# Sinkhorn attention and routed experts on one core: keys and scores of batches 2 to 4 issued in longer runs

## The chip, the core and the metric

The kernel runs on one NeuronCore of a Trainium2 chip. TensorE (PE) multiplies into PSUM, eight banks of 2 KB per partition; VectorE (DVE) and ScalarE (ACT) read PSUM and write SBUF, where operands live; GpSimd (POOL) works on SBUF and issues DMAs, and SyncE (SP) issues DMAs. Each engine takes its own instructions in order. The metric is the time of one execution on the device in microseconds (us), lower is better.

## The reference, cut to what matters

For each of 4 batches and 8 heads (768 positions, 64 dimensions, 8 blocks of 96), a normalised 8 x 8 matrix P sorts the blocks of keys and values; attention is then taken inside each block. The result, 3072 x 512, goes through 8 experts with weights from a Sinkhorn balance of the gate's logits.

```python
    for _ in range(5):
        P = P - np.max(P, axis=-1, keepdims=True)
        P = np.exp(P)
        P = P / (np.sum(P, axis=-1, keepdims=True) + 1e-09)
        P = P / (np.sum(P, axis=-2, keepdims=True) + 1e-09)
    k_sorted = np.einsum('bhij,bhjcd->bhicd', P, k_b).reshape(B, H, S, D)
    v_sorted = np.einsum('bhij,bhjcd->bhicd', P, v_b).reshape(B, H, S, D)
    scores = scale * np.matmul(q_b, k_sb.transpose(0, 1, 2, 4, 3))
    attn = np.exp(scores)                       # less the row's maximum
    attn = attn / (np.sum(attn, axis=-1, keepdims=True) + 1e-09)
    x = np.matmul(attn, v_sb)                   # then to 3072 x 512
    # experts: P from x @ w_gate, balanced 8 times over rows and columns
    for e in range(E):
        h = np.maximum(x @ w1[e], 0.0)
        out += P[:, e:e + 1] * (h @ w2[e])
```

## The kernel before, in words

The first batch (index 0 in the code) is done by its own code up to line 535. The other three go through `attention(bb, bank, plan)`, line 369: a generator that reads a string. Each word of the string is a step, and a step is one or more pieces joined by commas, a letter and a head pair (0 to 3):

- `q`, `queries` (174): turns a pair's queries on TensorE. Batch 2 (index 1) does it with 128*64 matmuls, one head into each half of the columns; batches 3 and 4 first have POOL reorder them into `qr`, two buffers (186), and use 128*128 matmuls. ACT copies the result to `qTs`; DVE does for pairs 2 and 3 of batch 2 and for pair 3 of batch 4 (193).
- `k`, `keys` (196): the sorted keys in two halves of three steps, each with one bank, 128*64 matmuls into both column halves; DVE copies each half to `kTs` (209).
- `s`, `scores` (218): four banks, 16 matmuls with 64 rows each, the two heads in the two row halves; ACT takes the exponent of each bank (234).
- `m`, `mix` (237): four banks of attention times sorted values (`vsb`); DVE takes reciprocals and products into `og` (247, 248).
- `t`, `turn` (252): turns `og` through one bank; DVE copies to `xtT` (258). `l`, `logits` (263): the gate. `x`: one subtraction of `sum_x(0)` on DVE (128).

All these matmuls are pinned in the order of the program on TensorE. The copies on DVE and ACT are not: the planner of the framework orders them by their data and gives each tile a bank of the pool `pa`, which has eight (547).

Between the steps TensorE works on the first expert for the batch before: `first_two` (556) yields a hidden step (four matmuls of 384 columns, one bank, Relu on ACT, 399) or half of an output tile (four matmuls of 512 columns into a bank that its second half shares, then a copy by ACT or DVE, 414). `run_both` and `weave` say how many of them follow each step. `sort_values` (162) makes the next batch's sorted values, two heads a step, and `hop` (155) sends them to `vsb` by eight DMAs, half on SP and half on POOL. `load_batch` (70) and `spread_r` (151) put the next batch's loads and its sort matrix on POOL.

After the attention the rest (lines 613 on) is the experts: the last two batches of expert 0 beside the balance, then experts 1 to 7.

Of the kernel before, what the change touches and what calls it, by code (L numbers as in the profile page):

```python
# [25 lines left out]
def kernel(  # L26
# [124 lines left out]
    def spread_r(bb):  # L151
        for _ in build_r(bb, nc.gpsimd, 4):
            pass

    def hop(bb, pieces=None):
        for eng, i, h0, n in pieces or [(nc.gpsimd if i % 2 and bb > 1 else nc.sync, i, 0, 8)
                                        for i in range(NB)]:
            (pin if bb == 0 else lambda ins: ins)(eng.dma_start(
                out=mkap(vsbt[bb % 2], [[VW, 96], [1, 65 * n]], off=i * 520 + 65 * h0),
                in_=vs[16 * i:16 * i + 16, :, h0:h0 + n].rearrange("p kk h d -> p kk (h d)")))  # L160

    def sort_values(bb, bank):
        for h in range(8):
            vps = bank([128, 384], F32)
            pin(nc.tensor.matmul(vps, Rt[bb][:, h].rearrange("p i c -> p (i c)"),
                                 vt[bb][:, h, :], start=True, stop=True))
            nc.scalar.copy(vs[:, :, h, 0:64], vps.rearrange("p (kk d) -> p kk d", d=64))
            if h % 2:
                yield
        hop(bb)  # L170
# [3 lines left out]
    def queries(bb, hp, bank):  # L174

        qps = bank([128, 6, 128], BF16)
        if bb < 2:

            for kk in range(6):
                for h in range(2):  # L180
                    pin(nc.tensor.matmul(qps[64 * h:64 * h + 64, kk, :],
                                         qt[bb][:, 2 * hp + h, kk * 64:kk * 64 + 64],
                                         Ibig, is_transpose=True, start=True, stop=True))
        else:
            qr = sp.tile([128, 6, 2, 64], BF16, name="qr", bufs=2)
            nc.gpsimd.tensor_copy(
                qr.rearrange("p kk h d -> p h kk d"),
                qt[bb][:, 2 * hp:2 * hp + 2].rearrange("p h (kk d) -> p h kk d", d=64))
            for kk in range(6):
                pin(nc.tensor.matmul(qps[:, kk, :], qr[:, kk].rearrange("p h d -> p (h d)"),  # L190
                                     Ibig, is_transpose=True, start=True, stop=True))
        qT[bb, hp] = sp.tile([128, 128, 6], BF16, name="qTs", bufs=4)
        (nc.vector.tensor_copy if bb == 1 and hp > 1 or bb == 3 and hp == 3 else nc.scalar.copy)(
            qT[bb, hp], qps.rearrange("p kk c -> p c kk"))

    def keys(bb, hp, bank):

        kT[bb, hp] = sp.tile([128, NB, 16, 6], BF16, name="kTs", bufs=4)
        for b in range(2):
            kps = bank([128, 3, 128], F32)  # L200
            for j in range(3):
                kk = 3 * b + j
                for h in range(2):
                    pin(nc.tensor.matmul(  # L204
                        kps[64 * h:64 * h + 64, j, :],
                        kt[bb][:, 2 * hp + h, kk * 64:kk * 64 + 64],
                        Rt[bb][:, 2 * hp + h].rearrange("p i c -> p (i c)"),
                        start=True, stop=True))
            nc.vector.tensor_copy(kT[bb, hp][:, :, :, 3 * b:3 * b + 3],
                                  kps.rearrange("p kk (i c) -> p i c kk", i=8))  # L210
# [7 lines left out]
    def scores(bb, hp, bank):  # L218

        for b in range(2):  # L220
            sps = [bank([128, 4, 96], F32) for h in range(2)]
            for j in range(4):
                i = 4 * b + j
                for h in range(2):
                    r = slice(64 * h, 64 * h + 64)
                    pin(nc.tensor.matmul(  # L226
                        sps[h][0:96, j, :],
                        kT[bb, hp][r, i].rearrange("p c kk -> p (c kk)"),
                        qT[bb, hp][r, 16 * i:16 * i + 16].rearrange("p c kk -> p (c kk)"),
                        start=True, stop=True))  # L230
            for h in range(2):
                if b == 0:
                    new_at(bb, hp, h)
                nc.scalar.activation(out=at[bb, hp, h][0:96, 4 * b:4 * b + 4],
                                     in_=sps[h][0:96], func=AF.Exp, scale=scale)
# [133 lines left out]
    def attention(bb, bank, plan):  # L369

        def step(what, hp):
            if what == "q":
                queries(bb, hp, bank)
            elif what == "k":
                keys(bb, hp, bank)
            elif what == "s":
                scores(bb, hp, bank)
            elif what == "t":
                turn(bb, hp, bank, nc.vector.tensor_copy)
            elif what == "x":  # L380
                next(x0)
            elif what == "l":
                logits(bb, bank, (0, 1, 2) if hp == 0 else (3,))
            else:
                for h in range(2):
                    mix(bb, hp, h, bank)

        for some in plan.split():
            for x in some.split(","):
                step(x[0], int(x[1]))  # L390
            yield
# [41 lines left out]
    with tc.tile_pool(name="ps0", bufs=4, space=bass.MemoryType.PSUM,  # L433
# [71 lines left out]
        for x in ("s00 k2 s01 k3 p s02 s03 m00 s10 m01 s11 m02 t00 m03 s12 m10 t01 s13 h00 m11 "  # L505
# [12 lines left out]
            elif x[0] == "g":  # L518
                b, g, t = *n, part[x[1:]]
# [26 lines left out]
    with ExitStack() as c2:  # L546
        pa = c2.enter_context(tc.tile_pool(name="pa", bufs=8, space=bass.MemoryType.PSUM,
                                           reuse_waits="tile"))
        bank1 = lambda shape, dt: pa.tile(shape, dt, name="bank", tag="bank")
        ebank = lambda: bank1([128, 512], F32)  # L550
        def by_turns(x, y):
            for a, b in ((x, y), (x, y)):
                yield next(a)
                yield next(b)

        def first_two():
            yield from hidden0(384, halves[1], ebank, range(2, 8))
            for c0, hTs in ((0, halves[0]), (384, halves[1])):
                o = [output0(c0, hTs, ebank, keep, (tt,)) for tt in range(3)]
                if c0 == 0:  # L560
                    yield from by_turns(o[0], o[1])
                    yield from o[2]
                else:
                    for one in o:
                        yield from one
            for c0 in (S, S + 384):
                hTs = mps.tile([128, 8, 384], BF16, name="hTs")
                yield from hidden0(c0, hTs, ebank)
                yield from output0(c0, hTs, ebank, keep)

        ex = first_two()

        def run(n):
            for _ in range(n):
                next(ex)

        def run_both(a, counts):
            for n in counts:
                next(a, 0)
                run(n)  # L580

        at1 = attention(1, bank1, "k0 k1 q0 q1 s0 k2 q2 k3 q3 s1 s2 s3 "
                                  "m0 m1,t0 m2,t1 m3,t2 t3,l0 l3")
        run_both(at1, (1, 1, 1, 0, 1, 0, 0, 1, 0, 1, 0, 2))
        load_batch(2, [(x, 0, 8) for x in "vkq"])
        spread_r(2)
        run_both(at1, (2, 1, 1, 1))
        run_both(sort_values(2, bank1), (1, 0, 1, 0, 1))
        run_both(at1, (1, 1))
        usual = "q0,q1,k0 q2,k1,s0 q3,k2,s1 m0 k3,s2 m1,t0 s3 m2,t1 m3 t2 t3,l0 l3"  # L590
        for bb, ns in ((2, (5, 3, 2, 4)), (3, (5, 4, 0, 5))):
            at1 = attention(bb, bank1, usual if bb == 3 else usual.replace(
                "q2", "q2,x0").replace("q3", "q3,x0").replace("t0", "t0,x0"))
            weave(at1, ex, 5, ns[0])
            if bb + 1 < B:
                load_batch(bb + 1, [(x, 0, 8) for x in "vkq"])
                spread_r(bb + 1)
            else:
                load_w1(1)
                sums = sum_w(1)  # L600
            weave(at1, ex, 3, ns[1])
            if bb + 1 < B:
                weave(sort_values(bb + 1, bank1), ex, 5, ns[2])
            else:
                for _ in sums:
                    pass
            weave(at1, ex, 4, ns[3])
        for _ in ex:
            pass
# [16 lines left out]
    def bank():  # L626
        return bk.tile([128, 512], F32, name="bk")
# [314 lines left out]
```

## Time and profile before

| | |
|---|---|
| median of 3 runs | 667.63 us (667.5 to 667.65) |
| profiled execution | 667.97 us |
| its span, first to last instruction | 666.2 us |
| TensorE busy | 658.0 us (99%), 5141 matmuls |
| DVE, ACT, POOL busy | 557.9 (84%), 300.3 (45%), 471.0 us (71%) |
| attention of batches 2 to 4 on TensorE | 36.13 us (first keys) to 106.68 us |
| experts after it | 106.68 us to the end |

The busy time of TensorE is the union of its matmuls' records; their ends are modelled, and a matmul's record is longer than the step from its start to the next one's. So work on TensorE is best read from starts. "128*64" in a row is the stationary operand: rows by columns of the array in use. A bracket at the end of a timeline row is the idle time ahead of it and what ended it.

### The profile page before, as it was taken

The numbers are of one execution on the slowest core, as the hardware profiler recorded it, in microseconds if no ns is written. First come the engines' busy times: TensorE is split into PE (matmuls) and PEld (weight loads), VectorE is DVE, ScalarE is ACT, GpSimd is POOL, SyncE is SP. The second block draws the span as 40 slices with busy tenths as digits, with TensorE's granted clock in tenths as the row PEclk, the third lists the DMA queues.
The fourth block names the chain that finished last, engine by engine and source line by source line (L and its number), as shares of the span: only waits on it lengthen the run. The fifth ranks groups of instructions, "written<-read, shape, count | busy, mean of one in ns | idle before, by whom it ended". The sixth has DMA issues, their size and how long they took to land.

```text
span 666.2 us, 13218 instructions
## 1 busy us (share of the span) xinstructions
PE 658.0 (99%) x5141; PEld 435.5 (65%) x5141; DVE 557.9 (84%) x1128; ACT 300.3 (45%) x535; POOL 471.0 (71%) x500
## 2 busy tenths in 40 slices
PE   7999999999999999999999999999999999999997
PEld 3766675554666666666666666666666666666666
DVE  6656876785888898998989898988998989898996
ACT  5775773476455443333334333433343334333430
POOL 4813353037897998898897999689886999646652
PEclk9999999999999999999999999999999999999999
DMA  9998964003041240033103040034003130001124
GB/s 188 172 220 143 150 110 64 1 1 63 1 64 16 49 64 1 0 64 44 21 1 64 1 64 2 1 63 64 1 1 65 16 50 1 1 0 62 68 95 159
DMA packets 33375, 36.96 MB, mean 55 GB/s; under 512 B 2112, under 2 KB 26400, under 8 KB 33312
## 3 DMA queue, kind: packets, MB, share of 16 engines
q0 software_dynamic: 26784, 27.03, 25.9%
q1 hardware_dynamic: 6416, 8.99, 4.3%
q8 instruction: 40, 0.66, 0.4%
q14 instruction: 23, 0.19, 0.1%
q10 hardware_dynamic: 112, 0.10, 0.1%
HBM read 52.45 MB, written 6.29 MB: 88 GB/s over the span
## 4 chain that ended last, share of the span: by engine, by line
PE 95%; DVE 2%; DMA 1%; ACT 0%; issue 0%; POOL 0%; ACTq 0%; DVEq 0%; POOLq 0%
PE bk L694 38%; PE oacc L781 38%; PE bk L397 3%; PE bank L406 3%; PE oacc L406 3%; PE bank L397 2%; PE bank L244 1%; PE pair L365 1%; PE bank L204 1%; PE bank L226 1%; PE bk L781 1%; PE bank L255 1%; DMA vsb<-vs 1%; PE bk L817 1%; DVE vs L283 0%; PE bank L190 0%
## 5 line engine op out<-in xcount | busy, mean ns | idle before, releaser
L746 DVE SCALAR_TENSOR_TENSOR osbl<-oacc,glog,osbl 128x256 f32<-128x256 f32 (+1 forms) x490 | 255.7, 524 | 27.9 <-PE oacc L781 18.2
L764 POOL TENSOR_TENSOR hs<-hT 128x512 bf16<-128x512 bf16 (+2 forms) x105 | 98.6, 951 | 72.3 <-DVE hT L712 72.2
L694 PE MATMUL bk<-xtT,w1e 128*128 128x512 bf16 x504 | 148.6, 379 | 0.0
L712 DVE CUSTOM_DVE_ANT_0 hT<-bk,p 128x512 bf16<-128x512 f32 x168 | 116.1, 691 | 26.7 <-PE bk L694 23.5
L781 PEld LDWEIGHTS <-hT 128*128 128x128 bf16 x996 | 97.4, 98 | 62.6 <-issue 0.2
L781 PEld LDWEIGHTS <-hs 128*128 128x128 bf16 x996 | 97.4, 98 | 61.2 <-issue 1.6
L781 PE MATMUL oacc<-w2e,hT 128*128 128x256 bf16 x796 | 119.7, 273 | 0.0
L717 ACT COPY p<-bk 128x512 f32<-128x512 f32 x84 | 49.3, 587 | 147.4 <-PE bk L694 147.0
L764 POOL TENSOR_TENSOR hs<-hs,hT 128x512 bf16<-128x512 bf16 (+2 forms) x105 | 99.6, 958 | 4.5 <-ACT hT L739 0.2
L764 POOL TENSOR_TENSOR hs<-hT,hs 128x512 bf16<-128x512 bf16 (+2 forms) x105 | 99.1, 952 | 4.7
L694 PE MATMUL bk<-xc,wc 128*128 128x512 bf16 x336 | 99.8, 379 | 0.0
L739 ACT ACTIVATE hT<-bk 128x512 bf16<-128x512 f32 x84 | 50.2, 597 | 96.1 <-PE bk L694 96.1
L781 PE MATMUL oacc<-w2e,hs 128*128 128x256 bf16 x612 | 91.8, 273 | 0.0
L694 PEld LDWEIGHTS <-w1e 128*128 128x128 bf16 x672 | 65.7, 98 | 12.1
L740 DVE SCALAR_TENSOR_TENSOR h<-bk,hT 128x512 bf16<-128x512 f32 x84 | 57.2, 681 | 3.9 <-ACT hT L739 3.9
L712 DVE CUSTOM_DVE_ANT_0 hT<-bk,u 128x512 bf16<-128x512 f32 x84 | 58.0, 690 | 2.5 <-PE bk L694 2.5
L721 ACT COPY u<-bk 128x512 f32<-128x512 f32 x84 | 49.2, 586 | 23.8 <-PE bk L694 23.2
L726 ACT COPY p<-bk 128x512 f32<-128x512 f32 x84 | 49.3, 587 | 23.4 <-PE bk L694 23.4
L694 PEld LDWEIGHTS <-wc 128*128 128x128 bf16 x504 | 49.3, 98 | 8.0 <-issue 0.2
L781 PE MATMUL oacc<-w2s,hs 128*128 128x256 bf16 x364 | 53.3, 272 | 0.0
L694 PE MATMUL bk<-xtT,wc 128*128 128x512 bf16 x168 | 50.0, 379 | 0.0
L694 PE MATMUL bk<-xc,w1e 128*128 128x512 bf16 x168 | 50.0, 379 | 0.0
(149 smaller groups left out, 791.4 us busy)
## 6 DMA issues: line engine op xcount, KB each, us to landing
w1e<-in_moe_w_dram POOLq DMA_DIRECT2D x7, 1024.0 KB, 8.1
w2e<-in_moe_w_dram POOLq DMA_DIRECT2D x7, 1024.0 KB, 8.9
out_dram<-osbl SPq DMA_DIRECT2D x23, 256.0 KB, 2.0
kvq<-in_v_dram POOLq DMA_DIRECT2D x3, 768.0 KB, 10.6
kvq<-in_k_dram POOLq DMA_DIRECT2D x3, 768.0 KB, 11.5
vsb<-vs SPq DMA_DIRECT2D x18, 97.5 KB, 4.6
kvq<-in_q_dram POOLq DMA_DIRECT2D x4, 384.0 KB, 10.2
kvq<-in_q_dram POOLq DMA_DIRECT2D x2, 768.0 KB, 20.2
```

The lines of the kernel that those rows point to most:

```text
L397: pin(nc.tensor.matmul(hps[:, 0:384], w1t[0][:, kk, fb * 128:(fb + 1) * 128], xtT[:, kk, c0:c0 + 384], start=(kk == 0), stop=(kk == 3)))
L406: pin(nc.tensor.matmul(oacc, hTs[:, fb, tt * 128:(tt + 1) * 128], w2t[0][:, fb, :], start=(fb == 0), stop=(fb == 7)))
L694: hold(nc.tensor.matmul(ps, wa[:, kk, :], xa[:, kk, :], start=(first and kk == 0), stop=(kk == 1), skip_group_check=True))
L712: nc.vector._custom_dve(TENSOR_ADD_SAT, out=out, in0=ps, in1=other, s0=TOP, s1=0.0)
L717: still(nc.scalar.copy(p1, u))
L721: still(nc.scalar.copy(u2, u))
L726: still(nc.scalar.copy(p5, v))
L739: still(nc.scalar.activation(out=c21, in_=u, func=AF.Relu))
L740: nc.vector.scalar_tensor_tensor(out=h3[e, p][:, i, :], in0=u, scalar=0.0, in1=c22, op0=ALU.max, op1=ALU.subtract)
L746: nc.vector.scalar_tensor_tensor(out=o, in0=ps, scalar=glog[:, t, e:e + 1], in1=o, op0=ALU.mult, op1=ALU.add)
L764: hold(nc.gpsimd.tensor_tensor(out=c, in0=a, in1=b, op=o))
L781: nc.tensor.matmul(ps, h[:, fb, :], w[:, fb, :], start=(first and fb == 0), stop=(fb == 3), skip_group_check=True)
```

## The change

The plans, the strings, are rewritten, and a few counts with them.

- Batch 2: one hidden step goes ahead of the first keys. Then the keys of all four pairs and two queries in one step; the other two queries and the scores of two pairs in one; the scores of the other two. Before, most pieces had a step of their own with expert work between.
- Of the first expert's first half tile row, the first halves of all three output tiles (`by_turns` now takes any number) stand ahead of the first mix, then the second halves; before, two tiles went in turns and the third after them. The counts behind the later steps and in the sorting of batch 3's values are lowered to fit, so that all in all as much expert work lies in each batch as before.
- Batches 3 and 4: keys of pairs 0 and 1 in a run, keys 2 and 3 followed by scores 0 and 1 in a run, scores 2 and 3 in a run after mix 1; mix 2 and mix 3 move back by a step and turn 3 follows mix 3 and turn 2 closer. A step `-` does nothing and only leaves its place to expert work. The `x` pieces go with the same letters as before.

What is computed, and by how many instructions, stays.

```diff
+            elif what == "-":
+                pass
...
-        def by_turns(x, y):
-            for a, b in ((x, y), (x, y)):
-                yield next(a)
-                yield next(b)
+        def by_turns(*some):
+            for _ in range(2):
+                for one in some:
+                    yield next(one)
...
                 if c0 == 0:
-                    yield from by_turns(o[0], o[1])
-                    yield from o[2]
+                    yield from by_turns(*o)
...
-        at1 = attention(1, bank1, "k0 k1 q0 q1 s0 k2 q2 k3 q3 s1 s2 s3 "
+        at1 = attention(1, bank1, "k0,k1,k2,k3,q0,q1 q2,q3,s0,s1 s2,s3 "
                                   "m0 m1,t0 m2,t1 m3,t2 t3,l0 l3")
-        run_both(at1, (1, 1, 1, 0, 1, 0, 0, 1, 0, 1, 0, 2))
+        run(1)
+        run_both(at1, (2, 2, 4))
         load_batch(2, [(x, 0, 8) for x in "vkq"])
         spread_r(2)
-        run_both(at1, (2, 1, 1, 1))
-        run_both(sort_values(2, bank1), (1, 0, 1, 0, 1))
-        run_both(at1, (1, 1))
-        usual = "q0,q1,k0 q2,k1,s0 q3,k2,s1 m0 k3,s2 m1,t0 s3 m2,t1 m3 t2 t3,l0 l3"
+        run_both(at1, (3, 1, 1, 1))
+        run_both(sort_values(2, bank1), (1, 0, 1, 0, 0))
+        run_both(at1, (1, 0))
+        usual = "q0,q1,k0,k1 q2,q3 k2,k3,s0,s1 -0 m0 m1,t0 s2,s3 t1 m2 m3,t2 t3,l0 l3"
```

## The prediction

> **What bounds the kernel now.** Times are in us, durations from the one profiled execution. I read the page first (busy shares, chain), then TensorE's timeline around the attention of batches 2 to 4, then what ACT and DVE do beside it.
>
> ```profile
> PE 658.0 (99%) x5141; PEld 435.5 (65%) x5141; DVE 557.9 (84%) x1128; ACT 300.3 (45%) x535; POOL 471.0 (71%) x500
> ...
> PE 95%; DVE 2%; DMA 1%; ACT 0%; issue 0%; POOL 0%; ACTq 0%; DVEq 0%; POOLq 0%
> ```
>
> TensorE is the bound: 99% busy, 95% of the chain. So what the change does to TensorE's order counts in full, a saved switch as well as a new wait. Two stretches of TensorE's timeline (start, length, engine, line, operation), from batch 3 and from batch 2, show what it saves:
>
> ```profile
> 64.27 0.53 PE L204 MATMUL bank<-R,kvq 128*64 128x128 bf16 x12
> 64.73 0.82 PE L397 MATMUL bank<-xtT,w1e 128*128 128x384 bf16 x4
> 65.39 0.50 PE L190 MATMUL bank<-Ibig,qr 128*128 128x128 bf16 x6
> 65.82 0.53 PE L204 MATMUL bank<-R,kvq 128*64 128x128 bf16 x12
> 66.28 0.56 PE L226 MATMUL bank<-qTs,kTs 64*96 64x96 bf16 x16
> 66.77 0.82 PE L397 MATMUL bank<-xtT,w1e 128*128 128x384 bf16 x4
> 67.43 0.50 PE L190 MATMUL bank<-Ibig,qr 128*128 128x128 bf16 x6
> ```
> ```profile
> 42.04 0.50 PE L181 MATMUL bank<-Ibig,kvq 128*64 128x128 bf16 x12
> 42.37 0.50 PE L204 MATMUL bank<-R,kvq 128*64 128x128 bf16 x12
> 42.80 0.82 PE L397 MATMUL bank<-xtT,w1e 128*128 128x384 bf16 x4
> 43.56 0.53 PE L181 MATMUL bank<-Ibig,kvq 128*64 128x128 bf16 x12
> ```
>
> Read the starts. Twelve 128*64 matmuls between others of their own form take 0.33 (42.04 to 42.37); alone, 0.46 (64.27 to 64.73). Four L397 take 0.66 ahead of a 128*128 form (66.77 to 67.43), 0.76 ahead of a 128*64 one (42.80 to 43.56). So leaving the full form for the column halves and coming back costs 0.10 + 0.13 = 0.23, two switches. A batch's keys, scores (L226, row halves: 0.49 against 16 starts of which 8 are a pair, 8 x 0.045 = 0.36) and back cost 0.10 + 0.13 + 0.13 = 0.36, three switches. About 0.115 each.
>
> What the change risks is seen at the one place where before runs two pairs of scores in a row:
>
> ```profile
> 45.26 1.10 PE L226 MATMUL bank<-qTs,kTs 64*96 64x96 bf16 x25
> 46.54 0.34 PE L226 MATMUL bank<-qTs,kTs 64*96 64x96 bf16 x7 [0.18 <-ACT hTs L399]
> 46.92 0.59 PE L406 MATMUL bank<-w2e,hTs 128*128 128x512 bf16 x2
> ```
> ```profile
> 44.49 1.62 ACT L234 ACTIVATE atp<-bank 96x384 bf16<-96x384 f32 x4 [0.33 <-PE bank L226]
> 45.99 0.50 ACT L399 ACTIVATE hTs<-bank 128x384 bf16<-128x384 f32 x1
> 46.36 3.17 ACT L234 ACTIVATE atp<-bank 96x384 bf16<-96x384 f32 x8
> ```
>
> They take 1.66 from 45.26 to 46.92 where 0.49 + 0.36 = 0.85 would do: 0.81 of waiting for PSUM banks. The pool `pa` has eight; two pairs of scores take all eight, and ACT frees one per 0.38 (1.62 for four of 0.49).
>
> **The switches removed.** Counted from the plans: batch 2 has 16 switches before and 7 after; batches 3 and 4 have 13 each before, 7 after. 42 against 21. By form: eight runs keys-scores, six keys or queries alone and three scores alone before (8 x 0.36 + 6 x 0.23 + 3 x 0.23 = 4.95); three of each after (2.46). Saved: 2.4 to 2.5.
>
> [...] The rows of 0.10 and 0.13 are taken.
>
> **The waits added.** TensorE is in order, so I walked its order after the change with these prices, all starts to starts: hidden step 0.65 (L397), half output 0.86, queries and keys 0.33 per pair, scores 0.36, mix 0.72, turn 0.34, plus the switches. On the other side, a bank comes free after: key half on DVE 0.58, one per 0.49; query 0.81 on ACT (one per 0.70) or 0.94 on DVE; exponent or Relu 0.50 on ACT, one per 0.38; mix: all four banks 2.24 after its first matmul (48.65 to 50.89); turn 0.55. A copy starts about 0.3 after its last matmul starts. The n-th bank asked for needs the (n - 8)th one given back. The same walk over the order of before gives the attention's end at 106.45 where the trace has 106.68; the 0.23 is the wait in the first keys below.
>
> One run in full, batch 4, time zero at its first query. q0, q1 to 0.67; k0, k1 from 0.76 to 1.45; hidden from 1.55; q2, q3 2.21 to 2.88; hidden to 3.53; k2, k3 3.62 to 4.31; scores s0 from 4.41. Banks given back: q0 1.39, k0 1.78 and 2.27, q1 2.09, k1 2.76 and 3.25, hidden 2.90, q2 3.60, q3 4.09 (DVE), hidden 4.23, k2 4.64 and 5.12, first exponent 5.40, k3 5.61, exponent 5.78. s0 asks for the 15th to 18th bank and has the 10th back at 4.23: no wait. s1 is there at 4.81 and needs the 12th, 5.12: 0.37. Its second half at 5.36 needs the 14th, 5.61: 0.31. Together 0.68: DVE empties four key halves in 1.95 where TensorE fills them in 0.67. The same walk gives 0.57 in batch 2 and 0.68 in batch 3. Sum 1.9.
>
> The second runs, s2 and s3. In batch 2 it comes two hidden steps behind the first; ACT still owes eight exponents and two Relus, ten times 0.38, from 42.7 on, and the last bank is the second Relu's at 46.4: 1.2 of waits (0.81 before, with less ahead of it). In batches 3 and 4 mixes lie between: 0.5 and 0.2. Sum 1.8.
>
> Data and copies, in TensorE's way by the closer packing.
>
> Batch 2's queries: heads 0 to 3 are issued at 25.48 and land after 13.1, 38.58; heads 4 to 7 at 26.23 and 14.9, 41.1. Before, TensorE asks at 38.77 and 42.04; after, with all keys in front and fewer switches, at 38.16 and 40.77. The DMA shares stay, so it waits: 0.9.
>
> Batch 3's queries: the reordered copies (L186, 0.84 each) have two buffers, so the third and fourth come after q0, q1 on POOL, behind the four DMAs of the hop of the sorted values (2.14 at 62.04). Sorted values now end 1.8 ahead of q0 where it was 3.5, and q2, q3 are asked for in one step: 0.7. Behind them on POOL stand the loads of batch 4 (65.69 before), some 1.3 later; they land at 81.8 + 1.3, asked for past 86: hidden. SP's four hop DMAs land by 67.7 before; the first mix, past 70, hides them.
>
> Mixes: t0 now follows m1 with one hidden step after m0: 0.72 + 0.65 + 0.72 = 2.09 against 2.24 and the semaphore: 0.23, in batches 3 and 4. m3, t2, half output, t3: 0.72 + 0.34 + 0.86 = 1.92 against 2.24 plus a DVE keep ahead (0.69): 0.5 with the logits that wait for t2's copy. Sum with both batches 1.7.
>
> Waits after: 1.9 + 1.8 + 0.9 + 0.7 + 1.7 = 7.0. Waits before, from the rows: 0.81 in the score run, 0.21 in the first keys (36.13 to 36.80 where 0.46 would do), 0.26 in three small ones: 1.3. The first keys' wait goes, since a hidden step now covers the keys' landing. The three first halves ahead of m0 need the sorted values, landed at 47.6, and the first half of w2, at 45.2; TensorE is there past 47: nothing lost. The x0 differences and load_w1 move with their steps: DVE and POOL have room there.
>
> Sum: 7.0 - 1.3 - 2.4 = +3.3. Against the profiled execution, 667.97 (span 666.2 and 1.8 around it), 671.3; the median of the runs is 0.34 lower, so **670.9**.
>
> What the trace of before can't show is which bank the planner hands out. Taken: the one free longest. Lower bound: no bank wait at all, 3.7 less. Upper: each of the six score runs waits for one eviction more, 6 x 0.4 = 2.4 more: 673.3. The one row of this kind (0.81, walked as 0.85) is nearest to what I take.
>
> **The rivals.** First, evictions keep pace: only TensorE's instructions are pinned in these steps; if ACT and DVE free the banks of the six score runs ahead of need, the 3.7 there goes: 670.9 - 3.7 = 667.2, not slower. For it: from 63.5 to 69.4 queries, keys and scores run without a wait. Against: there each pair of scores has 2.0 to itself, and the run at 45.26 waited. It decides against me from 2.0 of that 3.7 on (below that the time stays over 668.97).
>
> Second, all waits, those for data and mixes too, lie in slack: then the switches alone remain, 667.63 - 2.4 = 665.2. Against: TensorE has no slack (7.00 busy of the 7.00 from 63, 10.00 of the 10.00 from 86), and the query landings are fixed by the DMA queue.
>
> Third, the clock: TensorE's granted clock is 1.00 from 36 to 47, waits of up to 0.38 included. If it fell to half over each first score run and the two steps behind it (2.0 of work), that adds 2.0 three times: 677. [...]
>
> Fourth, a switch is worth half of its price in the rows: 670.9 + 1.2 = 672.1. Against: the rows of 0.10 and 0.13 repeat within 0.01 at every switch from 41 to 106. [...]
>
> **How the numbers follow.** Forecast 0.67, first rival 0.13, second 0.12, third or a worse order of banks 0.05, fourth 0.03. A change under 0.2% (1.34) can't be told from none. Slower (over 668.97): 0.67 + 0.05 + 0.03 = 0.75; same: 0.13; faster: 0.12. The range leaves out the second rival and the worst of the third: 666.8 to 673.3.
>
> **What would show it.** Right: 21 switches; L226 in the first run of each batch taking 1.3 to 1.5 for 32 instead of 0.85; L181 at 38.6 released by the queries' DMA; L190 held by POOL in batch 3; the hidden step that follows attention (L397 into `bk`) starting near 110.0 and not at 106.68, and the same distance kept to the end. Wrong: that start before 107, or score runs of 0.85.

## The result

| | before | after |
|---|---|---|
| median | 667.62 us (667.5 to 667.65, 6 runs) | 670.59 us (670.35 to 671.82, 6 runs) |
| profiled execution, its span | 667.97, 666.2 us | 670.49, 668.7 us |
| attention of batches 2 to 4 on TensorE | 70.63 us | 73.48 us |

The change makes the kernel slower by a factor of 1.0048 (95% interval 1.0035 to 1.006). Forecast was 670.9 (666.8 to 673.3). The attention is counted from where the gate's matmuls ahead of it end by their starts, 36.05 before (the first keys start at 36.13) and 35.71 after. Lines of `attention` and behind it are two higher in the kernel after: its L399 is the L397 of before, L401 the L399, L408 the L406.

### The profile page after: what moved, and what is told of

It is laid out like the page before. It is cut to its first block, busy times and chain, and to the rows that moved or that the text cites. A ratio compares the mean times of both kernels' runs of the same rounds, so it can differ in the third digit from the quotient of the medians.

```text
span 668.7 us, 13140 instructions
## 1 busy us (share of the span) xinstructions
PE 654.6 (98%) x5065; PEld 435.7 (65%) x5141; DVE 558.4 (83%) x1128; ACT 300.1 (45%) x535; POOL 470.3 (70%) x500
## 4 chain that ended last, share of the span: by engine, by line
PE 93%; DVE 4%; ACT 1%; issue 1%; DMA 0%; ACTq 0%; DVEq 0%
PE oacc L783 38%; PE bk L696 37%; PE bk L399 3%; PE oacc L408 3%; PE bank L408 3%; PE bank L399 2%; PE bank L244 1%; PE pair L365 1%; DVE kTs L209 1%; PE bank L255 1%; PE bk L783 1%; PE bk L819 1%; PE bank L226 0%; ACT atp L234 0%; DVE xc L128 0%
## 5 line engine op out<-in xcount | busy, mean ns | idle before, releaser
L696 PE MATMUL bk<-xtT,w1e 128*128 128x512 bf16 x477 | 143.1, 379 | 1.0
L696 PE MATMUL bk<-xc,wc 128*128 128x512 bf16 x317 | 95.7, 379 | 0.4
L696 PEld LDWEIGHTS <-w1e 128*128 128x128 bf16 x672 | 65.8, 98 | 12.1
L696 PEld LDWEIGHTS <-wc 128*128 128x128 bf16 x504 | 49.3, 98 | 7.9 <-issue 0.2
L696 PE MATMUL bk<-xc,w1e 128*128 128x512 bf16 x160 | 48.2, 379 | 0.4
L696 PE MATMUL bk<-xtT,wc 128*128 128x512 bf16 x158 | 47.8, 379 | 0.0
```

Of the source, the lines that this page charges most:

```text
L696: hold(nc.tensor.matmul(ps, wa[:, kk, :], xa[:, kk, :], start=(first and kk == 0), stop=(kk == 1), skip_group_check=True))
```

## The profile after

First the page: busy time of the engines, and the shares of the chain that ended last.

```profile
PE 654.6 (98%) x5065; PEld 435.7 (65%) x5141; DVE 558.4 (83%) x1128; ACT 300.1 (45%) x535; POOL 470.3 (70%) x500
...
PE 93%; DVE 4%; ACT 1%; issue 1%; DMA 0%; ACTq 0%; DVEq 0%
```

TensorE's share of the chain falls from 95% to 93% and DVE's rises from 2% to 4%: something now ends TensorE's idle time on the vector side. (This profile lacks 76 records of matmuls, 64 of them at L696 in the later experts and 10 at L408, so TensorE's busy sum is not to be compared with that of before. Starts are.)

Next, the same view of both kernels: TensorE from the first step of a batch's attention to the first of the next, batches 2, 3 and 4. Columns: the stretch and its length, then each engine's busy time and count, TensorE's granted clock, DMA share and rate. Before:

```profile
36.05:63.51 27.46, 27.22 (x367) 17.28 (x363) 15.41 (x48) 16.82 (x38) 4.33 (x7) 1.00 1.04 176
63.51:85.84 22.33, 22.33 (x321) 15.65 (x320) 16.98 (x50) 16.08 (x37) 10.67 (x15) 1.00 0.98 160
85.84:106.68 20.84, 20.84 (x314) 14.74 (x312) 16.30 (x49) 12.03 (x27) 12.24 (x12) 1.00 0.38 68
```

After:

```profile
35.71:62.83 27.12, 26.30 (x364) 17.55 (x365) 14.97 (x47) 16.62 (x38) 2.91 (x4) 1.00 1.02 173
62.83:87.70 24.87, 23.10 (x326) 15.62 (x324) 17.92 (x51) 16.21 (x37) 12.13 (x17) 1.00 0.94 155
87.70:109.19 21.49, 21.21 (x311) 14.83 (x312) 16.22 (x49) 11.92 (x27) 12.22 (x12) 1.00 0.35 59
```

Batch 2 is 0.34 shorter, batch 3 is 2.54 longer, batch 4 0.65 longer: 2.85 in all. The stretches begin where they do by each execution's own start, 0.34 earlier in the one of after, so the span differs by 2.5. The rest, from the first `bk` step to the end of the span, is 559.5 in both: nothing is made up or lost later. The clock is 1.00 throughout.

TensorE's timeline of batch 3 after shows what took the time (start, length, engine, line, operation; in brackets the idle time ahead and what ended it):

```profile
64.38 0.82 PE L399 MATMUL bank<-xtT,w1e 128*128 128x384 bf16 x4
65.96 0.51 PE L190 MATMUL bank<-Ibig,qr 128*128 128x128 bf16 x6 [0.76 <-POOL qr L186]
66.72 0.51 PE L190 MATMUL bank<-Ibig,qr 128*128 128x128 bf16 x6 [0.25 <-POOL qr L186]
67.07 0.81 PE L399 MATMUL bank<-xtT,w1e 128*128 128x384 bf16 x4
67.81 0.86 PE L204 MATMUL bank<-R,kvq 128*64 128x128 bf16 x24
68.60 0.83 PE L226 MATMUL bank<-qTs,kTs 64*96 64x96 bf16 x17
69.70 0.80 PE L226 MATMUL bank<-qTs,kTs 64*96 64x96 bf16 x15 [0.26 <-DVE kTs L209]
70.43 0.82 PE L399 MATMUL bank<-xtT,w1e 128*128 128x384 bf16 x4
```

Two waits stand here. Four L399 take 0.66 by their starts, but the next step starts 1.58 behind (64.38 to 65.96), and the six L190 that should take 0.34 take 0.76 to the next six: 0.92 + 0.42 = 1.34 of waiting for POOL's reordered queries. Then 32 matmuls of scores take 1.83 (68.60 to 70.43) where 0.85 would do: 0.98.

POOL's side of the first wait:

```profile
58.79 1.59 POOL L186 COPY qr<-kvq 128x768 bf16<-128x768 bf16 x2 [21.75 <-DVE og L248]
62.92 2.16 POOL L158 DMA_DIRECT2D vsb<-vs  x4 [2.55 <-issue]
65.06 1.60 POOL L186 COPY qr<-kvq 128x768 bf16<-128x768 bf16 x2
```

The hop stands ahead of the third and fourth copy, and it begins 0.64 behind the last sorted value, which ACT has written at 62.28.

The chain that ended last does not go through this wait, though. Its pieces in the same stretch (start, length, what):

```profile
63.99 1.99 DVE kTs L209 x4
65.97 1.26 DVE xc L128
67.25 1.43 DVE xc L128
68.68 1.44 DVE kTs L209 x3
70.16 0.34 PE bank L226 x7
```

DVE copies the keys of pairs 0 and 1, then does two x0 subtractions, then empties the banks of keys 2 and 3, and the last scores start behind that. The operands of these scores, s0 and s1, had been ready long before 68.60: the keys of pairs 0 and 1 at 65.98 (DVE), their queries at 64.91 (ACT). So this wait is for banks and not for operands.

Batch 2 has the second run with no mix ahead of it:

```profile
43.56 0.71 PE L226 MATMUL bank<-qTs,kTs 64*96 64x96 bf16 x17
44.45 0.58 PE L226 MATMUL bank<-qTs,kTs 64*96 64x96 bf16 x8 [0.18 <-ACT atp L234]
45.21 0.34 PE L226 MATMUL bank<-qTs,kTs 64*96 64x96 bf16 x7 [0.18 <-ACT hTs L401]
45.59 0.81 PE L399 MATMUL bank<-xtT,w1e 128*128 128x384 bf16 x4
```

It takes 2.03, 1.18 too long; ACT's exponents and Relus end its waits, and the chain that ended last runs through ACT from 41.66 to 45.55. All six runs by the same reading: 1.39 and 2.03 in batch 2, 1.83 and 1.40 in batch 3, 1.45 and 1.29 in batch 4. Less 0.85 each that is 4.29 of waiting.

The account: switches 42 to 21, 2.4 saved at 0.115 each; score runs 4.29, POOL 1.34, mixes and turns about 1.0 of waits; waits of before gone, 1.3. That is +2.9, against +2.85 measured.

## The experiments

Theory: in runs of two score pairs the eight banks run out, because DVE and ACT empty them more slowly than TensorE fills them (batch 3 after: DVE takes 1.97 from 68.61 for four key halves that TensorE fills in 0.79, ACT 3.14 from 69.07 for eight banks of scores that 0.85 would fill); POOL is late in batch 3 because the sorting of its values moved; switches save 0.115 each. Each run below stood beside runs of the kernel before on its chip (medians 667.60 to 667.67).

### Batch 2's part alone

```diff
-        usual = "q0,q1,k0,k1 q2,q3 k2,k3,s0,s1 -0 m0 m1,t0 s2,s3 t1 m2 m3,t2 t3,l0 l3"
+        usual = "q0,q1,k0 q2,k1,s0 q3,k2,s1 m0 k3,s2 m1,t0 s3 m2,t1 m3 t2 t3,l0 l3"
```

> Only batch 2 has the new plan (with the sorting of batch 3's values two steps later and the first output halves in turns); batches 3 and 4 keep the old one. 33 switches of TensorE's mode against 42. My theory (banks of PSUM run out in runs of two score pairs, POOL is late with the reordered queries of batch 3 because the sorting ends later, switches save 0.115 each): batch 2 itself 0.3 shorter than before (27.1 against 27.5) when its queries land early as in the profiled run of the change, up to 0.5 longer when they land late; batch 3 longer by 0.65 to 1.3 in the wait of its queries (L190) for POOL, although its plan is the old one; batch 4 as before. Total 0.3 to 1.3 over before, near 668.1. Rival (batch 3's loss is made by its own plan, by score runs and keys): no wait for POOL, batch 3 as before, total 667.3.

Measured: 669.11 (668.54 to 670.65), profiled at 670.65. TensorE, in batch 2 and then in batch 3:

```profile
36.55 1.53 PE L204 MATMUL bank<-R,kvq 128*64 128x128 bf16 x48
38.95 0.86 PE L181 MATMUL bank<-Ibig,kvq 128*64 128x128 bf16 x24 [0.87 <-DMA kvq<-in_q_dram]
39.74 1.47 PE L399 MATMUL bank<-xtT,w1e 128*128 128x384 bf16 x8
42.05 0.86 PE L181 MATMUL bank<-Ibig,kvq 128*64 128x128 bf16 x24 [0.83 <-DMA kvq<-in_q_dram]
...
66.11 0.82 PE L399 MATMUL bank<-xtT,w1e 128*128 128x384 bf16 x4
68.03 0.51 PE L190 MATMUL bank<-Ibig,qr 128*128 128x128 bf16 x6 [1.09 <-POOL qr L186]
```

Two things are settled. Batch 3 waits 1.26 for POOL (66.11 to 68.03 instead of 0.66) with its old plan, so that wait belongs to the moved sorting, not to the regrouped queries; the rival, 667.3, is out. My own 0.3 to 1.3 over before was too low as well, it is 1.5: the wait for POOL lies at the top of its range and the late landing cost more than I allowed. And here the queries of batch 2 landed at 38.9 and 42.0, where the profile of the change had 37.1 and 39.1: TensorE lost some 1.9 to it by the starts (where I had it make batch 2 at most 0.5 longer). Without it the profiled time would be 668.7, near the lowest of the runs, 668.54. The new order has no slack for that landing, and whether it costs anything differs from execution to execution.

### Batches 3 and 4 alone

The plan `usual` of the change in the kernel before, whose batch 2 sorts earlier.

```diff
-        usual = "q0,q1,k0 q2,k1,s0 q3,k2,s1 m0 k3,s2 m1,t0 s3 m2,t1 m3 t2 t3,l0 l3"
+        usual = "q0,q1,k0,k1 q2,q3 k2,k3,s0,s1 -0 m0 m1,t0 s2,s3 t1 m2 m3,t2 t3,l0 l3"
```

> Only batches 3 and 4 have the new plan, batch 2 the old one with its earlier sorting. 30 switches. My theory: no wait of L190 for POOL above 0.2, but the four score runs of batches 3 and 4 wait 0.4 to 1.0 each and the mixes and turns 1.0 in all, against 12 switches less (1.4): attention 1.9 to 2.4 longer, total near 669.7. Rival (the wait for POOL belongs to the new plan of batch 3, which asks for two query pairs in one step): the wait of 1.3 is there too and the total is 670.5. Rival (the waits come from late operands, keys copied just ahead of the scores, and not from banks): the same time here, but the score pairs standing apart, in the next run, do not help.

Measured: 670.22 (670.03 to 670.57), between my 669.7 and the rival's 670.5. No L190 waits, as forecast, but the first score run of batch 3 is the worst of all, 2.53 (67.63 to 70.16), 1.68 of it waiting, where I had 0.4 to 1.0:

```profile
67.63 0.66 PE L226 MATMUL bank<-qTs,kTs 64*96 64x96 bf16 x16
68.96 0.20 PE L226 MATMUL bank<-qTs,kTs 64*96 64x96 bf16 x1 [0.67 <-DVE kTs L209]
69.42 0.80 PE L226 MATMUL bank<-qTs,kTs 64*96 64x96 bf16 x15 [0.26 <-DVE kTs L209]
70.16 1.47 PE L399 MATMUL bank<-xtT,w1e 128*128 128x384 bf16 x8
```

DVE, which should empty the banks of keys 2 and 3 (filled from 66.84), is at two x0 subtractions first:

```profile
66.28 0.67 DVE L128 TENSOR_TENSOR xc<-xtT 128x1024 bf16<-128x1024 bf16 x1
66.98 1.43 DVE L128 TENSOR_TENSOR xc<-xtT,xc 128x1024 bf16<-128x1024 bf16 x1
68.33 1.97 DVE L209 CAST kTs<-bank 128x384 bf16<-128x384 f32 x4
```

So the wait for POOL and the wait for banks are not independent costs: with POOL early TensorE reaches the banks sooner and waits there 1.68 instead of 0.98. Batch 3 is 0.64 shorter than with the whole change (24.23 against 24.87), and by the rows DVE accounts for that, not TensorE's wait for POOL: the first subtraction takes 0.67 here and took 1.34 there, beside POOL's late copies, and DVE is back at the keys 5.12 behind the batch's first query in place of 5.78.

### Scores one pair at a time

```diff
-        usual = "q0,q1,k0,k1 q2,q3 k2,k3,s0,s1 -0 m0 m1,t0 s2,s3 t1 m2 m3,t2 t3,l0 l3"
+        usual = "q0,q1,k0,k1 q2,q3 k2,k3,s0 s1 m0 m1,t0 s2 s3,t1 m2 m3,t2 t3,l0 l3"
```

> The change with the scores of batches 3 and 4 one pair at a time, with expert work between (keys stay in runs, the empty step goes). 29 switches, 8 more than the change. Bank theory: L226 for 16 matmuls takes 0.36 to 0.5 wherever it stands; the four score runs' 2.57 of waits in batches 3 and 4 fall below 0.5, the mixes' small waits stay, 8 switches cost 0.9: 1.1 under the change, 669.5. Operand theory (keys or queries are copied too late for the scores): s0 right behind k2, k3 still waits as the first run did, and the total stays within 0.4 of the change or goes over it, 670.6 to 671.5.

Measured: 669.30 (669.12 to 670.93), 1.3 under the change. The eight pairs take 0.63, 0.50, 0.65 and 0.49 in batch 3 and 0.49 each in batch 4: 0.3 of waits in place of 2.57. s0 right behind k2 and k3 takes 0.63, so late operands are not its cause. (For s1, which now stands later, this run alone would not tell; there the copies' times in the profile of the change do.) Eight switches more are paid for it, and it is still a gain.

### Four buffers for the reordered queries

```diff
-            qr = sp.tile([128, 6, 2, 64], BF16, name="qr", bufs=2)
+            qr = sp.tile([128, 6, 2, 64], BF16, name="qr", bufs=4)
```

> The change with four buffers for the reordered queries instead of two, so that POOL can reorder all four pairs ahead of the hop's DMAs. My theory: the 1.34 of waits of L190 for POOL in batch 3 go, but keys then come closer behind each other and the first score run waits some 0.3 more for banks: 0.7 to 1.1 under the change, near 669.6. Rival (the wait only moves to the next bank wait, as TensorE is held by DVE's copies of keys anyway): within 0.3 of the change. Rival (planner still puts the third and fourth copy behind the hop): no change, with L190 still released by POOL.

Measured: 681.35 (680.36 to 682.1), which none of the three had. POOL's timeline in batch 3, then TensorE's:

```profile
58.73 3.13 POOL L186 COPY qr<-kvq 128x768 bf16<-128x768 bf16 x4 [21.83 <-DMA kvq<-in_q_dram]
61.81 0.94 POOL L75 DMA_DIRECT2D kvq<-in_v_dram  x1
62.74 0.88 POOL L75 DMA_DIRECT2D kvq<-in_k_dram  x1
63.61 0.89 POOL L75 DMA_DIRECT2D kvq<-in_q_dram  x1
64.50 2.09 POOL L139 TENSOR_TENSOR R<-Pb,mask 128x512 bf16<-128x512 f32 x2
66.51 2.15 POOL L158 DMA_DIRECT2D vsb<-vs  x4
```
```profile
70.93 0.20 PE L244 MATMUL bank<-vsb,atp 96*96 96x65 bf16 x1
79.25 1.60 PE L244 MATMUL bank<-vsb,atp 96*96 96x65 bf16 x15 [8.12 <-DMA vsb<-vs]
80.67 1.47 PE L399 MATMUL bank<-xtT,w1e 128*128 128x384 bf16 x4
81.93 1.46 PE L244 MATMUL bank<-vsb,atp 96*96 96x65 bf16 x16
```

With two buffers the third copy has to wait for a matmul of the first (62.83 in the change), and the planner had the hop ahead of it. With four no copy waits: the planner put all four first, and then the next batch's three loads, 2.3 MB, and the sort matrix ahead of the hop; the hop's DMAs stood behind them, landing 4.6 to 12.7 after their issue, and the first mix waited 8.12 for sorted values. Why the planner chose this order is not shown. TensorE's granted clock was 1.00 from 60 to 71, 0.71 from 71 to 79, which lies in the wait, 0.50 from 79 to 83 with TensorE at work again, 0.80 from 83 to 87 and 1.00 from 87 to 92; four L399 took 1.26 (80.67 to 81.93) instead of 0.65. So the clock fell with this wait of 8.12. In the change, where the third rival of the prediction had it fall, and in batch 2's part alone with its waits of up to 1.26, it was 1.00 from 36 to 107.

Up to that mix the run bears out the one before it: no wait for POOL, 2.51 for the first score run, and the first mix 8.23 behind the first query in place of 8.91, so 0.68 gained of the 1.34. The first rival was right in that the wait moves on to the banks, if not in its size.

### The change again

The same kernel, nothing edited.

> The change itself once more, for the landing of batch 2's queries. If the forecast's wait for them is real but lies in the run-to-run spread of the DMAs (they landed 1.5 to 2.1 earlier in the first profile of the change than in the one of before), the times spread by 1 to 2 above a floor near 670.3, and a run over 671 would show L181 of batch 2 released by the queries' DMA; the kernel before has slack for it and spreads by 0.3. Rival (the wait is hidden whatever the landing): spread 0.3 and no such release.

Measured: 670.59 (670.38 to 671.44). The profiled execution shows no wait for the queries (L181 at 37.76 right behind the keys of 36.34), and the runs of before beside it spread as widely as the change's, which I had not expected; so the spread of times proves nothing here. What shows the wait is the profile of the first experiment, and a smaller one (0.36) in the run of the x0 subtractions below.

### Half of the late keys on ACT

```diff
-            nc.vector.tensor_copy(kT[bb, hp][:, :, :, 3 * b:3 * b + 3],
+            (nc.scalar.copy if bb > 1 and hp > 1 and b else nc.vector.tensor_copy)(kT[bb, hp][:, :, :, 3 * b:3 * b + 3],
                                   kps.rearrange("p kk (i c) -> p i c kk", i=8))
```

> The change with the second key half of pairs 2 and 3 in batches 3 and 4 copied by ACT instead of DVE; TensorE's order is untouched. If the first score run of a batch waits because DVE empties four key halves one behind the other, its time falls from 1.83 to about 1.4 in batch 3 and from 1.45 to about 1.05 in batch 4, less some 0.2 for exponents that ACT now takes later: total 0.5 to 0.8 under the change. Rival (ACT, not DVE, sets the pace of the banks in these runs): the runs get longer by one or two copies of 0.5, total 0.3 to 1.0 over the change.

Measured: 670.10 (from 669.95 on), 0.49 under the change. TensorE's order is the same; the first score run falls to 1.37 in batch 3 (68.61 to 69.98) and 1.25 in batch 4:

```profile
68.61 1.44 PE L226 MATMUL bank<-qTs,kTs 64*96 64x96 bf16 x32
69.98 1.48 PE L399 MATMUL bank<-xtT,w1e 128*128 128x384 bf16 x8
```

DVE's pace does hold these runs: with ACT and DVE emptying the banks together they are 0.46 and 0.20 shorter. Only batch 3 keeps it (24.45 in place of 24.87). In batch 4 ACT, with its exponents late, makes the first mix 0.28 longer, and the batch takes 21.49 as before; there the rival has its part.

### The x0 subtractions elsewhere

```diff
-                "q2", "q2,x0").replace("q3", "q3,x0").replace("t0", "t0,x0"))
+                "t0", "t0,x0").replace("-0", "x0").replace("t1", "t1,x0"))
```

> The change with two of batch 3's three x0 subtractions taken out of the step of queries 2 and 3 and put at the empty step and at turn 1. If DVE is late with the keys because the subtractions (1.34 and 1.43 instead of the 0.7 and 1.0 of before) stand in front of them, the first score run of batch 3 falls from 1.83 to the 1.45 of batch 4, which has none: 0.4 less in batch 3, total 0.2 to 0.4 under the change, and the subtractions take 0.7 and 1.0 again where POOL copies nothing beside them. Rival (POOL's late queries alone set the time there): no change of the run, and the subtractions cost as much in their new place.

Measured: 670.55 (from 670.00 on). The run in question takes 1.45 (69.05 to 70.50), just as forecast:

```profile
69.05 1.52 PE L226 MATMUL bank<-qTs,kTs 64*96 64x96 bf16 x32
70.50 1.47 PE L399 MATMUL bank<-xtT,w1e 128*128 128x384 bf16 x8
```

Batch 3 is 0.35 shorter, the subtractions take 0.84, 0.68 and 0.68, and the lowest run is 0.38 under that of the change. The median, 0.04 under the change's, does not show it; in the profiled execution batch 2's queries were late by 0.36.

### A new order, and the price of a switch

The walk over banks and copies from the prediction was used to look for an order with few switches and few waits. Every letter is a step as before; `e` is one step of the first expert, `S` two heads of the next batch's sorting, `L` the next loads, `W` the sums of the weights. The loop that reads the letters, in place of the counts, is left out here.

```diff
...
+        plans = (" e e k3 k0 e q0 k1 k2 q1 s0 e e e s1 q2 q3 e s2 e s3 e L m0 e m1 e t0 e e S e m2 e t1 m3 e S e t2 S t3 e S l0 l3",
+                 " e q0 k0 k3 q1 e s0 k1 k2 q2 e x0 e s1 q3 x0 e L m0 e s2 m1 t0 e m2 e s3 t1 e t2 S S e e m3 S e l0 t3 e x0 S l3 e",
+                 " q0 k3 k0 k2 k1 q1 e e s0 e q2 s1 q3 e e L m0 e e s2 m1 e t0 m2 e s3 t1 W e t2 m3 e e e t3 l0 e l3")
...
```

> A new order of the three batches, searched by hand of the same walk over banks and copies: keys in runs where DVE has time, scores one pair at a time (never two), 33 to 34 switches, the sorting of batch 3's values spread out earlier, the first mix where before has it. The walk puts the end of attention 1.9 ahead of before: 665.7 if banks, copies and switches are all there is to it. If switches are worth half of what the rows gave, 666.2; if waits that the walk does not know (POOL beside DVE, late DMAs) are left, 666.5 to 667.6.

Measured: 666.26 (from 666.09 on), ratio to before 0.9973 (0.9955 to 0.9991). Attention runs from 35.76 to 104.80: 69.04, against 70.63 before and 73.48 with the change, with 33 switches. The walk had 1.9 less than before and got 1.6; one wait of 0.4 is left, in the scores of pair 3 in batch 3.

Against this order, one with the keys of batches 3 and 4 taken apart, so that only switches are added:

```diff
-                 " e q0 k0 k3 q1 e s0 k1 k2 q2 e x0 e s1 q3 x0 e L m0 e s2 m1 t0 e m2 e s3 t1 e t2 S S e e m3 S e l0 t3 e x0 S l3 e",
-                 " q0 k3 k0 k2 k1 q1 e e s0 e q2 s1 q3 e e L m0 e e s2 m1 e t0 m2 e s3 t1 W e t2 m3 e e e t3 l0 e l3")
+                 " e q0 k0 q1 k3 e s0 e k1 q2 k2 x0 e s1 q3 x0 e L m0 e s2 m1 t0 e m2 e s3 t1 e t2 S S e e m3 S e l0 t3 e x0 S l3 e",
+                 " q0 k3 q1 k0 e k2 e k1 q2 s0 e q3 s1 e e L m0 e e s2 m1 e t0 m2 e s3 t1 W e t2 m3 e e e t3 l0 e l3")
```

> The order of the last run of the call before once more, on the same chip as the next two: 666.3.

> The order with few waits, with the keys of batches 3 and 4 put apart by expert steps that stood beside them, so that nothing waits longer but TensorE changes its tiling 44 times instead of 33. [...]

Measured side by side: 666.63 (from 666.21 on) and 668.19 (from 667.50 on). From the first step of batch 3 to the end of attention the profiles have 43.14 (first run of the order; 43.42 in the second, which waits 0.26 for POOL ahead of batch 4) and 44.64. Score steps that wait longer account for 0.29 of the 1.50, so eleven switches cost 1.2, 0.11 each. The lowest runs are 1.29 apart, 0.12 each, or 0.09 if those 0.29 are in them too. The price of the prediction, 0.115, which makes 1.3 of eleven, stands within that, and its fourth rival, half of it and 0.6, falls.

A last order, chosen so that the walk finds no bank wait even with seven banks:

```diff
+        plans = (" e e e e k2 k0 q0 q1 k1 e e s0 k3 q2 q3 s1 e s2 e s3 e L m0 e e m1 e e t0 e t1 S m2 e S m3 e S t2 S e t3 l0 e l3",
+                 " q0 q1 k2 k0 k1 e e s0 k3 e x0 q2 e x0 q3 e e L s1 e m0 e m1 e s2 e s3 t0 e m2 t1 e S m3 t2 e e S t3 l0 S S x0 l3",
+                 " q0 k0 k1 k2 q1 e e s0 k3 e e s1 q2 q3 e e L m0 e s2 m1 t0 e s3 e m2 e t1 e m3 t2 W e e t3 l0 e l3")
```

> A second order by the same walk, chosen so that it has no bank wait even with seven banks, the x0 subtractions away from the keys, and batch 2's queries and keys one hidden step later. The one wait of 0.4 left in batch 3 of the first order (scores of pair 3 at 74.4) should go; the walk gives the same end for the rest: 665.9. Rival (the walk's margin is not what was missing, and the second half of w2 that lands at 47 to 49 is asked for too early): 666.3 to 666.6.

Measured: 665.48 (665.24 to 666.83), ratio 0.9969 (0.9957 to 0.9981): 2.2 us faster than the kernel before and 5.1 faster than the change. The profiled execution was one of its longer ones, 666.34, and shows why:

```profile
43.11 0.56 PE L226 MATMUL bank<-qTs,kTs 64*96 64x96 bf16 x16
44.61 1.04 PE L408 MATMUL bank<-w2e,hTs 128*128 128x512 bf16 x3 [0.94 <-DMA w2e<-in_moe_w_dram]
```

No score step waits for a bank any more, all of batches 3 and 4 take 0.49; the first output step waits 0.94 for w2, its first half where the rival had the second. The other executions were not profiled: those near 665.3 are 1.0 shorter, as they would be without this wait, but that they lack it is not shown. The median is 0.4 under the walk's 665.9.

## Why the prediction was right, step by step

The time, the sign and the main cause came out: waits for banks eat more than the switches give. By the terms of the sum:

| term | forecast | measured |
|---|---|---|
| 21 switches saved | 2.4 to 2.5 | 1.9 to 2.5 (0.09 to 0.12 each, from eleven switches) |
| first score runs | 1.9 (0.57, 0.68, 0.68) | 2.12 (0.54, 0.98, 0.60) |
| second score runs | 1.8 (1.2, 0.5, 0.2) | 2.17 (1.18, 0.55, 0.44) |
| batch 2's queries landing | 0.9 | 0 in five profiles with this batch 2, the change's two among them; 1.9 and 0.4 in two others |
| batch 3's queries behind the hop | 0.7 | 1.34 |
| mixes and turns | 1.7 | 1.0 |
| waits of before | 1.3 | 1.3 gone |
| attention | +3.3 | +2.85 |

The sum is close because errors cancel: 0.9 and 0.7 too much for the landing and the mixes, 0.6 too little for POOL, 0.6 too little for the score runs. That much is luck. The mis-sized terms are these.

- The queries' landing was taken from one execution as a constant. It is a spread: 37.1 to 38.9 for the first half, 39.1 to 42.0 for the second, over the profiles of before, of the change and of batch 2's part alone. The wait is real (1.9 in batch 2's part alone), but the order has no slack rather than a fixed loss, and with the profiled execution's own data it cost nothing.
- POOL's term was too small: the hop's first DMA on POOL began at 62.92, 0.64 behind the last sorted value, where I had it at once, and both late queries then came one copy apart (0.92 and 0.42).
- Batch 3's first run, 0.98 for 0.68, had a neighbour that the walk did not price: I wrote that the x0 differences move with their steps and DVE has room. DVE had none: they took 1.34 and 1.43, stood ahead of the keys and lie on the chain that ended last. Moving them brought the run to 1.45.
- Mixes were over-priced by 0.7: t0 behind m1 lost 0.07 to 0.08, not 0.23.
- The walk treated waits as adding up. They overlap: taking POOL's 1.34 away gains 0.64 only, since DVE's chain of copies and subtractions runs beside it.
- That ACT sets the pace of the second runs is read from what ended their waits and from the chain; no run here changed ACT's pace alone.
- Two of its sums do not come out as written: 1.2, 0.5 and 0.2 make 1.9 and not 1.8, and 0.23 and 0.5 in two batches make 1.46 and not 1.7. The lower end of the range, 666.8, is 0.4 under 670.9 - 3.7 without a term for it. Each wait of the run shown in full has 0.06 in it that is not named. The forecast would move by 0.1.

Of the rivals, the first (evictions keep pace) is refuted by the 4.29 and by scores taken apart; the second by the same; the third by the clock of 1.00 in the change: of the profiles read from 36 to 107 only the one with the wait of 8.12 has less, 0.93; the fourth by the eleven switches, 0.09 to 0.12 each (its half was the author's estimate, and no run shows it). Of "what would show it": 21 switches, L190 held by POOL and the distance kept to the end came out; the first score runs took 1.39, 1.83 and 1.45 where I had 1.3 to 1.5; the `bk` step started at 109.19 rather than 110.0, since attention grew by 2.85 and not 3.3 and this execution reached it 0.34 earlier; and L181 was not released by the DMA in this profile.

## What to carry to other kernels

Work that shares a form is worth grouping only as far as the engines that empty PSUM keep up (here a switch saved was worth 0.09 to 0.12, and the six runs of two score pairs waited 4.29): count the banks that a run asks for and when the n-8th comes back, and stop the run there; here keys in runs and scores one pair at a time beat both kernels. Price a move by walking the in-order engines with durations from the trace, but give DMA landings a spread (39.1 to 42.0 for one load here) and leave slack for them. And before loosening a buffer, ask which other order it was holding: two buffers were what kept the hop ahead of 2.3 MB of loads.

## What was not expected of the hardware

- A subtraction of `x` on DVE (L128, 128x1024) took 0.68 with POOL idle (76.1 in the change); beside POOL's copies it took 1.34 (65.88 on, with POOL at its copies from 65.06 to 66.66). Beside POOL's DMA issues one took 1.43 (67.25 on, issues from 66.60 to 69.30), but another 0.69 in the kernel before (65.63 on, issues from 65.69, the last copy over at 65.77) and one 0.67 in batches 3 and 4 alone (66.28 on, issues from 65.39 to 68.08). What makes the difference is not shown.
- The same DMAs landed at different times in different executions. The two halves of batch 2's queries, issued at 25.48 and 26.23 before and at 25.35 and 26.12 in the change, landed at 38.58 and 41.1 before and at 37.1 and 39.1 in the change; in batch 2's part alone the matmuls that waited for them started at 38.95 and 42.05.
